# A two-expert kernel after windowed attention: the pools of PSUM banks are merged two feature ranges later

## Chip, cores, metric

The kernel runs on one core of a Trainium2 chip. The metric is device time in microseconds of one execution, the median of the runs shown. On the core, TensorE (PE) does matmuls and transposes into PSUM, VectorE (DVE) and ScalarE (ACT) read PSUM and do the elementwise work, GpSimd (POOL) and SyncE (SP) issue most of the transfers. Each engine takes its own instructions strictly in the order in which they were written to it, and waits on semaphores for the others.

## What is computed

```
scores = q @ k^T / 8, kept only where 0 <= i - j < 64       # 4 batches, 8 heads, 576 rows, 64 per head
x      = softmax(scores) @ v, heads side by side            # 2304 x 512
h      = x @ w_in ;  g = clamp-square of h ;  x2 = g @ w_out # 512 -> 2048 -> 512
h2     = x2 @ w_in2 ; solu = h2 * softmax(h2) ; layer norm, gain
out    = ln @ w_out2                                        # 512 -> 1024 -> 512
```

The function of h is (h + 1)^2 / 4 between -1 and 1, 0 below and h above. All is float32; the large products are made from three matmuls each of a high and a low part (hi*hi, hi*lo, lo*hi).

## The kernel before

The 2304 tokens are cut into six blocks of 384 (`NB`); a block is two attention tiles of 192 tokens, and a tile has four pairs of heads, so that a block needs eight attention units, numbered g. The first expert runs over the blocks j and, inside a block, over 16 ranges of 128 features, f. One step (j, f) is

- `moe_h` (L490): 12 matmuls of 384 columns that sum h for 128 features in one PSUM bank, tile `ps_h`, from the block's `xh` and `xl` (four chunks of 128 features of x, three matmuls each);
- `moe_g`, `moe_g2`, `moe_g3` (L500 to L515): ACT makes relu and square of it (L505, L506), DVE the clamp that reads the bank a last time (L511), ACT the high part `gh` (L512), DVE the low part `gl` (L515);
- `moe_y` (L518, L526): 12 matmuls, that add the step's contribution to the four sums `acc0` to `acc3` of the block, one bank each. After f = 15, `moe_out` copies the four sums out (`xo`, by ACT at L536 and DVE at L538) and POOL writes them to DRAM (L539); the copies have two buffers, so that the third and fourth wait until the first and second are written.

In this document h(j,f) and y(j,f) stand for the 12 matmuls of `moe_h` and of `moe_y`. The attention of later blocks is spread over the steps in small pieces (`slots`, L600): scores of a unit (`ps_s`, L352, and L442 in the form for two units together), their maximum by DVE (L360, L452), the exponential by ACT (L366, L458), the normalisation by DVE (L377, L378, L386), the transposes of the probabilities (`ps_p`, L402) with their copy by ACT (L407), and the product with v (`ps_x`, L421), which ACT and DVE turn into `xh` (L428) and `xl` (L429). Each of `ps_s`, `ps_p` and `ps_x` takes a PSUM bank for a while. Units 14 and 15 complete the x of block 1; their products with v run while the last steps of block 0 do.

PSUM has eight banks. Four are the sums. During block 0 the other four are two pools of two: `ps_at` for the attention pieces and `ps_h` for h. When these are closed, one pool `ps_ring` of four takes their banks, and attention pieces and h take turns in it; a tile of the new pool waits for what used its bank before. `at_bank` and `h_bank` (L95 to L106) take from the ring as soon as there is one.

The order on each engine isn't the order of the text: a list scheduler with a simulated time line places the instructions from their dependences, the banks among them, when the kernel is built. So a change of who may use which bank moves instructions.

Of the kernel before, what the change touches and what calls it, by code (L numbers as in the profile page):

```python
# [20 lines left out]
def kernel(  # L21
# [73 lines left out]
    def at_bank(name):  # L95
        if spare:
            spare.append(spare.pop(0))
            if spare[-1] is not None:
                return ps_acc.tile([128, 512], F32, tag=spare[-1], name=name)
        if ring:  # L100
            return ring[0].tile([128, 512], F32, tag="r", name=name)
        return ps_at.tile([128, 512], F32, tag="a", name=name)
# [47 lines left out]
    def w_conv(start=True):  # L150
        if w_b:
            split_c(*w_b.pop(0))
        if w_a:
            w_b.append(w_a.pop(0))
            split_b(*w_b[-1])
        if w_raw and start:
            w_a.append(w_raw.pop(0))
            split_a(*w_a[-1])
# [331 lines left out]
    def moe_h(j, f, c):  # L490
        ps = h_bank()[:, c]
        n = 0
        for kc in range(KC):
            hi, lo = wih[f][:, kc, :], wil[f][:, kc, :]
            for a, bb in ((hi, xh[j]), (hi, xl[j]), (lo, xh[j])):
                nc.tensor.matmul(ps, a, bb[:, kc, c], start=(n == 0), stop=(n == 3 * KC - 1))  # L496
                n += 1
        return ps

    def moe_g(part, ps):  # L500
        c = part[2]
        u = wk_p.tile([128, NB], F32, tag="u", name="u")[:, c]
        hi = wk_p.tile([128, NB], F32R, tag="gh", bufs=3, name="gh")[:, c]
        lo = wk_p.tile([128, NB], F32R, tag="gl", bufs=3, name="gl")[:, c]
        nc.scalar.activation(u, ps, ACTF.Relu, bias=half, scale=0.5)  # L505
        nc.scalar.activation(u, u, ACTF.Square)  # L506
        gh[part[0], part[1], part[2].start], gl[part[0], part[1], part[2].start] = hi, lo
        return ps, u, hi, lo

    def moe_g2(ps, u, hi, lo):  # L510
        g = nc.vector.scalar_tensor_tensor(u, u, 1.0, ps, op0=ALU.min, op1=ALU.max)  # L511
        return nc.scalar.copy(hi, u).ins, g.ins  # L512

    def moe_g3(j, ps, u, hi, lo):
        nc.vector.tensor_tensor(lo, u, as_f32(hi), op=ALU.subtract)  # L515
# [15 lines left out]
    def moe_out(j, es):  # L531
        for e in es:
            xo = wk_p.tile([128, NB], F32, tag="u" if j == NBLK - 1 and e > 1 else "xo", name="xo")
            a = acc.pop((j, e))[:, 0:NB]
            if e % 2 == 0:
                nc.scalar.copy(xo, a)  # L536
            else:
                nc.vector.tensor_copy(xo, a)  # L538
            nc.gpsimd.dma_start(out=x2d[j][e], in_=xo)  # L539
# [109 lines left out]
    def slot(n):  # L649
        for _ in range(n):  # L650
            next(stages, None)
# [7 lines left out]
    def x2_load(p):  # L659
        r = x2r[p] = d_p.tile([128, KC, 256], F32, tag="x2", bufs=2, name="x2r")  # L660
        c = 0
        while c < 256:
            j, c0 = divmod(256 * p + c, NB)
            n = min(256 - c, NB - c0)
            nc.sync.dma_start(out=r[:, :, c:c + n], in_=x2d[j][:, :, c0:c0 + n].rearrange("e p n -> p e n"))
            c += n
# [183 lines left out]
    for n in range(len(seq) + 2):  # L850
        if n < len(seq):
            j, f, c = seq[n]
            last = j == NBLK - 1
            n0 = n1 = 1
            if c == FIRST:
                z = na * (f + 1) // F0 - na * f // F0
                n0, n1 = z - z // 2, z // 2
            if j == 1 and f == 0:
                fr_ctx.close()
                ring.append(rg_ctx.enter_context(  # L860
                    tc.tile_pool(name="ps_ring", bufs=4, space=PSUM, reuse_waits="tile")
                ))
            if last and f == 8:
                rg_ctx.close()
                ring[0] = ps_ctx.enter_context(tc.tile_pool(name="ps_ring2", bufs=2, space=PSUM, reuse_waits="tile"))
            if last and f == 0:
                at_ctx.close()
                d_p = ctx.enter_context(tc.tile_pool(name="d", bufs=2, side="right", reuse_waits="tile"))
                x2_load(0)
            if j == 1 and f == 4:  # L870
                gl_row = wk_p.tile([128, NB], F32, tag="xo", name="gl_row")[0:DF2 // 128, 0:128]
                nc.sync.dma_start(
                    out=gl_row.rearrange("k (b i) -> k b i", b=4),
                    in_=g_ln.rearrange("(b k i) -> k b i", b=4, i=32),
                )
            if j == 1 and f == 7:
                ps = at_bank("ps_g")
                nc.tensor.transpose(ps[:, 0:DF2 // 128], gl_row, ident[0:DF2 // 128, 0:DF2 // 128])
                nc.vector.tensor_copy(gl_sb, ps[:, 0:DF2 // 128])
            part = moe_g(seq[n], moe_h(j, f, c))  # L880
        if n >= 1 and n - 1 < len(seq):
            moe_g3(seq[n - 1][0], *prev)
        if n < len(seq):
            prev = part
            slot(n0)
            w_conv()
            pins = moe_g2(*part)
        if n >= 2:
            jy, fy, cy = seq[n - 2]
            moe_y(jy, fy, cy)  # L890
            if fy == NF - 1:
                moe_out(jy, (0, 1))
        if n < len(seq):
            slot(n1)
            w_conv()
            if j == 0:
                w_load(2)
            w2_step(n, *pins)
            if last and f < 2:
                w2_vals(f)  # L900
            if last and f in (2, 3):
                w2_sums(f - 2)
            if last and f >= 2:
                with tc.issue_after(pins[0]):
                    w2_split(f - 2)
            if last and 2 <= f < 10:
                w2_load(f - 2)
        else:
            w_conv()
        if n >= 2 and fy == NF - 1:  # L910
            moe_out(jy, (2, 3))
        if n < len(seq):
            if last and f == 1:
                x2_load(1)
            if last and f == 5:
                with tc.issue_after(pins[0]), tc.issue_after(pins[1]):
                    x2_prep(0)
            if last and f in P_STEPS:
                st_p(0, P_STEPS[f])
            if last and f == 14:  # L920
                l2_norm(0)
            if last and f == 15:
                st_p(1, "P2")
        elif n == len(seq):
            x2_load(2)
            x2_prep(1)
            st_p(1, "P3")
            l2_norm(1)
# [66 lines left out]
```

## Time and profile before

| | us |
|---|---|
| median of 3 runs (703.43 to 706.93) | 703.74 |
| the profiled execution | 703.17 |
| its span on the core | 701.4 |
| PE busy | 678.1 (97%) |
| PE weight loads busy | 625.6 (89%) |
| DVE busy | 448.3 (64%) |
| ACT busy | 412.5 (59%) |
| POOL busy | 134.2 (19%) |

The profiled execution takes 1.8 us more than its span. Times below are from the start of the span. A busy PE is one that has a matmul in flight: matmuls overlap, so that the distance from one start to the next, not the length of one, tells how fast they go.

### The profile page before, as it was taken

To read this page: it belongs to the slowest core of one execution; us is meant where nothing else is said; L and a number is where in the kernel's file an instruction comes from. 1 tells how busy PE (TensorE), PEld (TensorE's weight loads), DVE (VectorE), ACT (ScalarE), POOL (GpSimd) and SP (SyncE) were. 2 spreads that over 40 slices of the span, in tenths; PEclk is the share of its full clock that TensorE was granted. 3 is DMA by queue.
4 is the path that set the end of the run, shared out by engine and by line. 5 is a ranking of instruction groups with operands and counts; after the bars stand their busy time and mean duration, and the time that the engine had idled before them with its cause. 6 is when DMAs were issued, how large, how long until landed. Compare 5 with 4: busy or idle time off the path is not lost.

```text
span 701.4 us, 12574 instructions
## 1 busy us (share of the span) xinstructions
PE 678.1 (97%) x4439; PEld 625.6 (89%) x4439; DVE 448.3 (64%) x1213; ACT 412.5 (59%) x1006; POOL 134.2 (19%) x178
## 2 busy tenths in 40 slices
PE   6899888899999999999999999999999999999998
PEld 5689788799999999999999999999997888888887
DVE  4789889646445555454455552643289999999850
ACT  5889777665656655665566565364455555445451
POOL 1112221100001000021112111662272322220000
PEclk9999999999999999999999999999999999999999
DMA  9996896625353523346351211562024455444331
GB/s 194 253 241 161 218 245 196 148 35 108 72 116 112 116 64 76 77 129 126 85 113 61 106 41 51 173 202 93 1 83 142 155 178 189 158 147 150 103 109 46
DMA packets 150551, 88.94 MB, mean 127 GB/s; under 512 B 118616, under 2 KB 134744, under 8 KB 150488
## 3 DMA queue, kind: packets, MB, share of 16 engines
q1 hardware_dynamic: 135160, 49.84, 30.2%
q0 software_dynamic: 12592, 33.57, 14.9%
q10 hardware_dynamic: 2736, 4.72, 1.8%
q8 instruction: 35, 0.57, 0.3%
q14 instruction: 28, 0.23, 0.1%
HBM read 63.97 MB, written 24.12 MB: 126 GB/s over the span
## 4 chain that ended last, share of the span: by engine, by line
PE 71%; issue 13%; POOL 4%; DVE 4%; DMA 3%; SPq 3%; ACT 2%; POOLq 0%; DVEq 0%
PE acc L526 21%; PE ps_h L496 21%; PE ps_o L827 14%; PE P L712 9%; DMA wst<-in_moe_w_in_dram 3%; POOL wil L249 2%; PE ps_x L476 2%; PE ps_s L442 2%; PE ps_p L402 2%; SPq L279 1%; DVE gl L515 1%; POOL wst L124 1%; SPq L302 1%; POOL wst L126 1%; DVE x2p L692 1%
## 5 line engine op out<-in xcount | busy, mean ns | idle before, releaser
L511 DVE SCALAR_TENSOR_TENSOR u<-u,ps_h 128x384 f32<-128x384 f32 (+1 forms) x98 | 53.3, 544 | 142.3 <-ACT u L506 141.4
L496 PE MATMUL ps_h<-xh,wih 128*128 128x384 f32 (+1 forms) x392 | 132.0, 337 | 3.1 <-ACT wih L145 3.0
L526 PE MATMUL acc<-gl,woh 128*128 128x384 f32 (+1 forms) x392 | 130.3, 334 | 2.1 <-DVE gl L515 2.1
L496 PE MATMUL ps_h<-xl,wih 128*128 128x384 f32 (+1 forms) x392 | 130.7, 334 | 0.4 <-DVE xl L429 0.4
L496 PE MATMUL ps_h<-xh,wil 128*128 128x384 f32 (+1 forms) x392 | 130.9, 334 | 0.0
L526 PE MATMUL acc<-gh,wol 128*128 128x384 f32 (+1 forms) x392 | 129.3, 332 | 0.0
L526 PE MATMUL acc<-gh,woh 128*128 128x384 f32 (+1 forms) x392 | 123.8, 341 | 2.3 <-ACT gh L512 2.3
L505 ACT ACTIVATE u<-ps_h,half 128x384 f32<-128x384 f32 (+1 forms) x98 | 56.1, 574 | 97.5 <-PE ps_h L496 97.3
L515 DVE TENSOR_TENSOR gl<-u,gh 128x384 fp32r<-128x384 f32 (+1 forms) x98 | 62.6, 640 | 35.2 <-ACT gh L512 34.6
L512 ACT CAST gh<-u 128x384 fp32r<-128x384 f32 (+1 forms) x98 | 49.7, 508 | 49.9 <-DVE u L511 34.8
L496 PEld LDWEIGHTS ps_h<-xh,wih 128*128 128x128 f32 x392 | 74.1, 189 | 4.5 <-ACT wih L145 3.6
L526 PEld LDWEIGHTS acc<-gh,woh 128*128 128x128 f32 x392 | 72.0, 188 | 6.2 <-ACT gh L512 3.5
L526 PEld LDWEIGHTS acc<-gl,woh 128*128 128x128 f32 x392 | 73.7, 188 | 3.1 <-DVE gl L515 2.7
L496 PEld LDWEIGHTS ps_h<-xl,wih 128*128 128x128 f32 x392 | 74.1, 189 | 1.0 <-DVE xl L429 0.8
L496 PEld LDWEIGHTS ps_h<-xh,wil 128*128 128x128 f32 x392 | 74.1, 189 | 0.1
L526 PEld LDWEIGHTS acc<-gh,wol 128*128 128x128 f32 x392 | 73.6, 188 | 0.1
L712 PE MATMUL P<-wih,x2p 128*128 128x512 f32 x216 | 71.6, 390 | 0.7 <-DVE x2p L692 0.7
L827 PE MATMUL ps_o<-woh,wol 128*128 128x512 f32 (+1 forms) x152 | 57.6, 379 | 0.0
L827 PE MATMUL ps_o<-woh,woh 128*128 128x512 f32 (+1 forms) x152 | 57.5, 379 | 0.0
L827 PE MATMUL ps_o<-wol,woh 128*128 128x512 f32 (+1 forms) x152 | 57.5, 378 | 0.0
L506 ACT ACTIVATE u<-u 128x384 f32<-128x384 f32 (+1 forms) x98 | 51.1, 522 | 1.9
L712 PEld LDWEIGHTS P<-wih,x2p 128*128 128x128 f32 x216 | 40.4, 188 | 9.2 <-DVE x2p L692 1.1
(123 smaller groups left out, 1191.8 us busy)
## 6 DMA issues: line engine op xcount, KB each, us to landing
wst<-in_moe_w_out_dram POOLq DMA_DIRECT2D x22, 512.0 KB, 7.4
wst<-in_moe_w_in_dram POOLq DMA_DIRECT2D x21, 512.0 KB, 5.5
vw<-in_v_dram SPq DMA_DIRECT2D x32, 256.0 KB, 5.3
lnd<-e SPq DMA_DIRECT2D x16, 512.0 KB, 2.7
lT<-lnd SPq DMA_DIRECT2D x64, 128.0 KB, 3.0
x2d<-xo POOLq DMA_DIRECT2D x24, 192.0 KB, 2.6
out_dram<-o ACTq DMA_DIRECT2D x17, 256.0 KB, 2.0
w2d<-w2st POOLq DMA_DIRECT2D x8, 512.0 KB, 3.0
```

The lines of the kernel that those rows point to most:

```text
L249: nc.gpsimd.tensor_tensor(lo, v_, as_f32(hi), op=ALU.subtract)
L402: nc.tensor.transpose(ps[:, i * 128:i * 128 + 128], p[:, i, :], ident)
L442: nc.tensor.matmul(ps[x][64 * c:64 * c + 64, i * 128 + c0:i * 128 + 128], z[r, KQ + i * 64:KQ + i * 64 + 64], z[r, i * 64 + c0:i * 64 + 12 ...
L496: nc.tensor.matmul(ps, a, bb[:, kc, c], start=(n == 0), stop=(n == 3 * KC - 1))
L505: nc.scalar.activation(u, ps, ACTF.Relu, bias=half, scale=0.5)
L506: nc.scalar.activation(u, u, ACTF.Square)
L511: g = nc.vector.scalar_tensor_tensor(u, u, 1.0, ps, op0=ALU.min, op1=ALU.max)
L512: return nc.scalar.copy(hi, u).ins, g.ins
L515: nc.vector.tensor_tensor(lo, u, as_f32(hi), op=ALU.subtract)
L526: nc.tensor.matmul(acc[j, e][:, c], a, bb, start=(f == 0 and n == 0 and c.start == 0), stop=(f == NF - 1 and n == 2),)
L712: nc.tensor.matmul(ps, l, r, start=(n == 0), stop=(n == 5))
L827: nc.tensor.matmul(ps, a[kk // 4][:, kk % 4, :], b[kk][:, c:c + w], start=(n == 0), stop=(n == 3 * NK2 - 1),)
```

## The change

The two pools of block 0 stay open for the steps (1,0) and (1,1); the ring of four is opened at (1,2).

```diff
-            if j == 1 and f == 0:
+            if j == 1 and f == 2:
                 fr_ctx.close()
                 ring.append(rg_ctx.enter_context(
                     tc.tile_pool(name="ps_ring", bufs=4, space=PSUM, reuse_waits="tile")
                 ))
```

No instruction is added or removed, and none changes its shape. The scheduler orders a stretch anew that begins at the last step of block 0 and ends with the transposes `ps_p_2129`; from there on the engines' orders are the same but for a swap of two neighbours on ACT and one on PE. Three places follow. In the names, `wih_146` and `wil_147` are the weights of f = 0, `wih_168` and `wil_169` those of f = 1, `woh_150` belongs to y(1,0), `wol_173` to y(1,1), `acc_751` to `acc_754` are the sums of block 0, `acc_2047` to `acc_2050` those of block 1.

PE before, from the scores of unit 16 on (the first row):

```order
L352 MATMUL ps_s<-kq_124 128x128 x3
L421 MATMUL ps_x<-pT,vw 64x64 x6
L402 MATMUL ps_p<-ident,p 128x128 x3
L352 MATMUL ps_s<-kq_125 128x128 x3
L496 MATMUL ps_h<-xh,wih_146 128x384
L496 MATMUL ps_h<-xl,wih_146 128x384
```

PE now, from the last of y(0,15) to the first of y(1,0); the transposes `ps_p` are those of the third row above:

```order
L526 MATMUL acc_754<-gh,wol_1409 128x384
L496 MATMUL ps_h<-xh,wih_146 128x384
L496 MATMUL ps_h<-xh,wih_168 128x384
L496 MATMUL ps_h<-xl,wih_146 128x384
L496 MATMUL ps_h<-xh,wil_147 128x384
L496 MATMUL ps_h<-xl,wih_168 128x384
L496 MATMUL ps_h<-xh,wil_169 128x384
L402 MATMUL ps_p<-ident,p 128x128 x3
L352 MATMUL ps_s<-kq_125 128x128 x3
L421 MATMUL ps_x<-pT,vw 64x64 x6
L526 MATMUL acc_2047<-gh,woh_150 128x384
```

Before, these transposes came right behind the scores and the product with v of another unit, with all of h(1,0) after them. Now the 24 matmuls of h(1,0) and h(1,1) are done ahead of them, 14 of these also ahead of the scores of the first row, and behind them come scores, a product with v and y(1,0).

ACT before, from the copy of the third sum of block 0 on:

```order
L536 COPY xo_2010<-acc2_753 128x384
L407 COPY pT_1825<-ps_p_1824 128x384
L366 ACTIVATE p_1831,sm_1833<-p_1831,mx_1832 128x128 x3
L505 ACTIVATE u_1861<-ps_h_1848,half_69 128x384
L428 CAST xh_1895<-ps_x_1897 128x192
```

ACT now, the same stretch:

```order
L536 COPY xo_2005<-acc2_753 128x384
L505 ACTIVATE u_1856<-ps_h_1843,half_69 128x384
L505 ACTIVATE u_1932<-ps_h_1919,half_69 128x384
L506 ACTIVATE u_1856<-u_1856 128x384
L506 ACTIVATE u_1932<-u_1932 128x384
L407 COPY pT_1825<-ps_p_1824 128x384
L512 CAST gh_1857<-u_1856 128x384
L366 ACTIVATE p_1831,sm_1833<-p_1831,mx_1832 128x128 x3
```

The copy `pT_1825`, which the product `ps_x` waits for, stood first and now stands behind four operations on h.

PE now, from the end of y(1,1) on, with the transposes and the product with v of unit 17:

```order
L526 MATMUL acc_2050<-gh,wol_173 128x384
L402 MATMUL ps_p<-ident,p 128x128 x3
L421 MATMUL ps_x<-pT,vw 64x64 x6
L442 MATMUL ps_s<-kq_124 64x128
L442 MATMUL ps_s<-kq_125 64x128
```

Before, h(1,1) stood between these transposes and this product, and the first ten matmuls of y(1,0) between the pair scores (`ps_s`, L442) and h(1,2). Now nothing stands between any of them. The scores go on for ten more rows, those of tile `ps_s_1947` first and those of `ps_s_1948` behind; then follows h(1,2) with `ps_h_2016`, the first tile of the ring, which waits for DVE, while the second, `ps_h_2073`, waits for nothing. On DVE the three maxima of `ps_s_1947` come first, then a transpose of q and k (L317), then the three of `ps_s_1948`.

## Rows read from the trace of the kernel before

**Rows 1.** Windows: PE, PEld, DVE, ACT, POOL busy us (instructions), clock, DMA share, GB/s.
```profile
130.00:134.00 4.00, 1.65 (x22) 1.35 (x21) 2.89 (x12) 2.06 (x9) 1.24 (x4) 1.00 0.84 207
```

**Rows 2.** Waits of PE from 145 us to the end: us, times, longest.
```profile
PE acc L526 <- DVE gl L515: 1.3, 1, 1.3
PE P L712 <- DVE x2p L692: 0.7, 1, 0.7
```

**Rows 3.** Timeline of PE around the gap: start, us, what, [idle before].
```profile
129.40 0.83 PE L352 MATMUL ps_s<-kq 128*128 128x128 f32 x6
130.16 0.71 PE L421 MATMUL ps_x<-pT,vw 64*64 64x64 f32 x12
133.23 0.52 PE L402 MATMUL ps_p<-ident,p 128*128 128x128 f32 x3 [2.35 <-DVE p L386]
133.58 0.83 PE L352 MATMUL ps_s<-kq 128*128 128x128 f32 x6
134.32 0.44 PE L496 MATMUL ps_h<-xh,wih 128*128 128x384 f32 x1
```

**Rows 4.** Timeline of DVE and of ACT in and behind the gap.
```profile
132.52 0.56 DVE L386 TENSOR_TENSOR p<-p,rs 128x384 f32<-128x384 f32 x1
...
133.78 0.48 ACT L407 COPY pT<-ps_p 128x384 f32<-128x384 f32 x1 [1.34 <-PE ps_p L402]
```

**Rows 5.** Timeline: last matmul of h(1,0) on PE, then ACT behind it.
```profile
136.33 0.34 PE L496 MATMUL ps_h<-xh,wil 128*128 128x384 f32 x1
...
136.71 0.58 ACT L505 ACTIVATE u<-ps_h,half 128x384 f32<-128x384 f32 x1 [0.65 <-PE ps_h L496]
137.22 0.32 ACT L428 CAST xh<-ps_x 128x192 fp32r<-128x192 f32 x1
137.43 0.53 ACT L506 ACTIVATE u<-u 128x384 f32<-128x384 f32 x1
137.86 0.47 ACT L407 COPY pT<-ps_p 128x384 f32<-128x384 f32 x1
```

**Rows 6.** Timeline of DVE, a stretch without idle time.
```profile
140.71 0.36 DVE L429 TENSOR_TENSOR xl<-ps_x,xh 128x192 fp32r<-128x192 f32 x1 [1.03 <-ACT xh L428]
141.14 0.55 DVE L511 SCALAR_TENSOR_TENSOR u<-u,ps_h 128x384 f32<-128x384 f32 x1
141.61 0.64 DVE L317 STREAM_TRANSPOSE kq<-qk 128x448 f32<-128x448 f32 x1
142.17 0.25 DVE L452 CUSTOM_DVE_ANT_0 p<-ps_s,mask 128x128 f32<-128x128 f32 x1
...
143.41 0.55 DVE L515 TENSOR_TENSOR gl<-u,gh 128x384 fp32r<-128x384 f32 x1
```

**Rows 7.** Timeline of PE: transposes, a product with v, pair scores of two units.
```profile
137.21 0.52 PE L402 MATMUL ps_p<-ident,p 128*128 128x128 f32 x3
...
139.75 0.57 PE L421 MATMUL ps_x<-pT,vw 128*64 128x64 f32 x12
140.25 0.89 PE L442 MATMUL ps_s<-kq 64*64 64x128 f32 x24
```

**Rows 8.** Timeline of PE: first matmul of h(1,2); transposes behind h(1,4).
```profile
142.91 0.33 PE L496 MATMUL ps_h<-xh,wih 128*128 128x384 f32 x1
...
151.58 0.82 PE L402 MATMUL ps_p<-ident,p 128*128 128x128 f32 x6
```

**Rows 9.** Sums of block 0: copy (ACT), write (POOL); landings, issues 129.4 and 132.7.
```profile
128.56 0.48 ACT L536 COPY xo<-acc 128x384 f32<-128x384 f32 x1 [0.52 <-PE acc L526]
131.98 0.46 ACT L536 COPY xo<-acc 128x384 f32<-128x384 f32 x1
...
129.44 1.10 POOL L539 DMA_DIRECT2D x2d<-xo  x2 [13.14 <-ACT xo L536]
...
DMA to landing us min/median/max: 2.2/2.2/2.2
...
DMA to landing us min/median/max: 5.1/5.1/5.1
```

**Rows 10.** Windows near the start, columns as in rows 1.
```profile
30.00:33.30 3.30, 1.83 (x20) 1.14 (x19) 2.75 (x8) 3.30 (x12) 0.00 (x0) 0.95 1.09 175
33.30:36.30 3.00, 3.00 (x23) 2.83 (x23) 2.13 (x7) 2.98 (x9) 0.54 (x1) 0.50 0.53 79
```

## The prediction

> **What bounds the kernel.** I read the page first: PE is busy for 97% of the span, so whatever stops PE moves the end, and whatever doesn't is hidden. Next I read where PE waits. From 145 us to the end it waits twice, for 1.3 and 0.7 us [rows 2]; a delay that PE has at 145 us can be given back nowhere but there. Then the stretch that the change orders anew. In 130 to 134 us PE is busy for only 1.65 us [rows 1], and the timeline shows why: the product with v starts at 130.16, and the transposes behind it start at 133.23 after an idle 2.35 us [rows 3]. They wait for DVE's normalisation, which runs from 132.52 and ends at 133.08 [rows 4]. The 12 matmuls of h(1,0) stand behind these transposes in PE's order, since their bank is the one that the transposes fill: h starts at 134.32, just after ACT has emptied that bank (133.78 + 0.48 = 134.26) [rows 3, 4]. This is the only large gap of PE in the stretch.
>
> **What the change removes.** With the old pools open, h(1,0) and h(1,1) have two banks of their own, so that the 24 matmuls no longer queue behind the transposes. One matmul costs 0.1734 us: 50 of them fill 142.91 to 151.58 [rows 8]. Counted along the new order, the scores that stood at 129.40 have 14 matmuls of h put ahead of them and 3 of y(0,15) put behind, net 11 x 0.1734 = 1.91 us; with 0.2 for four more changes between small and large matmuls (a first large matmul behind small ones starts its successor 0.28 later and not 0.17: 134.32 in rows 3 is followed at 134.60) they start at 131.5. From these scores to the transposes the chain through DVE and ACT took 133.23 - 129.40 = 3.83 us [rows 3], so the transposes can start at 135.33. PE meanwhile does the product with v (starts 0.76 behind the scores [rows 3], takes 0.65) and 13 large matmuls (2.26 us and 0.1), until 135.27. The gap of 2.35 shrinks to 0.06. Gain: **2.3 us**.
>
> By the Trainium skill's page Perfetto Trace Analysis, section Optimization Strategy, a gap that repeats on the engine that should be busy can mean that too little PSUM is there for the next tile. By that rule the sum would end here, at 703.17 - 2.3 = 700.9; here the gap comes once, and what ends it is DVE and not a freed bank, so I count on.
>
> **What the change adds.** The 24 matmuls were the cover of the steps behind. I follow the new order with durations from the rows.
>
> 1. *Product with v of unit 16.* PE has transposes at 135.33 and the scores of unit 17 0.35 later, which take 0.74 [rows 3], and is ready for the product at 136.42. It needs ACT's copy of the transposes, now behind four operations. The last matmul of h(1,0) starts at 134.75, that of h(1,1) at 135.10; ACT starts relu 0.38 behind a last matmul (136.33 to 136.71), the next operation follows relu after 0.51 and square after 0.43 [rows 5]. So relu at 135.13 and 135.64, square at 136.15 and 136.58, the copy at 137.01 to 137.48, the product at 137.54 (+0.06 as in rows 3 and 4). PE idles **1.12 us**.
> 2. *Low part of g(1,0).* The product ends at 138.05; three matmuls of y(1,0) use the high part and end at 138.65. The fourth needs DVE's low part. DVE's order is clamp (after the square, 136.71), three maxima, a transpose, the clamp of h(1,1), the low part. Its pitches are 0.47 for a clamp, 0.56 for the transpose, 0.62 for three maxima (half of 142.17 to 143.41), 0.55 for the low part [rows 6]: 136.71 + 0.47 + 0.62 + 0.56 + 0.47 + 0.55 = 139.38. PE idles **0.75 us**. Then 21 matmuls of y run through, 3.64 us, to 143.07; their other inputs are ready a microsecond before they are needed.
> 3. *Product with v of unit 17.* It stands directly behind its transposes (143.15). ACT's copy starts 0.65 behind these and takes 0.47 (137.21, 137.86 [rows 5, 7]), so the product starts at 144.33, where the transposes were done at 143.5. PE idles **0.8 us**; before, h(1,1) filled this.
> 4. *Pair scores.* The first tile's scores follow after 0.5 (139.75 to 140.25 [rows 7]) and take 0.41. The second tile's bank is that of the product, which DVE leaves 140.71 + 0.36 - 139.75 = 1.32 after its start [rows 6, 7], at 145.65. PE idles **0.45 us**.
> 5. *h(1,2).* In the two attention banks, taken in turn, the transposes that h(1,0) waited for before, the product of unit 17 and the second tile of pair scores share one. That bank is the ring's first again, and h(1,2) waits for DVE, h(1,3) for nothing: it is the second tile's maxima that h(1,2) waits for. DVE starts 0.43 behind the start of its low part of x (145.29 + 0.43 = 145.72), then three maxima, a transpose, three maxima: 0.62 + 0.56 + 0.62, until 147.52, with a hand-over of 0.06 147.58. PE was done with the scores at 146.1 and idles **1.5 us**; before, ten matmuls of y(1,0) stood there.
>
> From there 36 matmuls of h (6.24 us and 0.1) bring PE to the transposes of unit 18 at 153.9; it was there at 151.58 with the same work done [rows 8]. That is 2.3 later; by the waits, 0.06 + 1.12 + 0.75 + 0.8 + 0.45 + 1.5 = 4.7 of new idle time against 2.35 of old, also **+2.3 us**. The small swaps behind this stand beside PE's work and cost nothing as long as PE doesn't wait there [rows 2]. Transfers on SP (queries, keys and v of later units) are issued some 2 us later; their units come several steps later, so that nobody waits for them. POOL's four writes of block 0's sums move too (rival D).
>
> Each of the new waits has 0 below. Step 1 can grow by a late write of the sums (up to 2.5, rival D), steps 2 to 5 by little, since each is a chain of measured pieces.
>
> **Sum.** 703.17 (profiled execution) + 2.3 = 705.5; that execution lies 0.57 below the median of three, against which it would be 706.0. I say 705.8.
>
> **Rivals.**
> - *B, the gap goes and the new waits don't come.* 703.17 - 2.35 = 700.8 at best, about 703 with half of the waits. For it: each wait is short, and ACT and DVE are far from full in the stretch. Against it: in steps 1, 3 and 5 PE's next instruction reads or overwrites just what the chain makes.
> - *C, the clock falls.* From 143.5 to 147.6 PE works for some 1.3 us and idles in three pieces. Near the start PE was busy for 1.83 of 3.3 us, and in the 3.0 us behind, at full work, its granted clock was 0.50, that is 1.2 in place of 2.4 GHz [rows 10]. Against it: in 130 to 134 us, with 1.65 busy of 4, the clock stayed at 1.00 [rows 1]. If it fell, 3.0 us of full work at half speed cost 1.5: 705.5 + 1.5 = 707.0. The Trainium skill's TensorE: Matmul & The Clock Gate, section A second HAM failure mode: psum-queue depth-cycling, says that a PE that idles briefly between groups while cycling through PSUM banks swings between the two clock levels. The trace has both outcomes.
> - *D, the sums' write lands late (slower).* The third sum's copy on ACT waits until the first is in DRAM, and now relu of h(1,0) and all of step 1 stand behind this copy. The first copy started 0.84 ahead of the scores (128.56, 129.40 [rows 3, 9]); three matmuls fewer stand between now, 0.52, so it starts at 131.18, and POOL issues 0.88 behind its start (129.44 [rows 9]), at 132.06. Landing took 2.2 us for this write and 5.1 for the third, that was issued into the loads of v [rows 9]. These loads reuse buffers that the product of unit 15 frees: it began 0.72 behind the issue before (130.16), 0.2 behind it now (132.26). With 2.2 the write is there at 134.26; the third copy, which stood 2.58 behind the scores (131.98) and could go at 134.08, ends at 134.72, 0.4 before relu. With 5.1 it ends at 137.16 + 0.46 = 137.62, relu is 2.5 late and so is step 1: 705.5 + 2.5 = 708.0. It costs something from a landing of 2.6 on, and puts the time over half a per cent from 4.4 on.
> - *E, nothing moves the end.* The waits are as long as the gap: 703.2 to 704.2. It needs half of the new waits to be hidden, and I see no cover for them.
>
> **Numbers.** Half a per cent, 3.5 us, is what a measurement of this kernel can tell from no change. Forecast 0.62, B 0.08, C 0.12, D 0.08, E 0.10. Of D half, of C a third and a little of the forecast's upper end lie above 707.3: slower 0.12. Faster needs under 700.2, more than the whole gap: 0.02. Same: 0.86. The range of 8 in 10 leaves out B, and the upper half of D: 703.4 to 707.5.
>
> **What would show it.** Right: the wait of the transposes for DVE's normalisation gone, and PE waiting in 136 to 148 us for ACT's copy of the transposes (twice, about 1.1 and 0.8), for DVE's low part of g (0.8), and before h(1,2) for DVE's maxima (1.5), with the transposes behind h(1,4) near 153.9 and everything later shifted by that. Wrong: those transposes at 149 (B), a granted clock under 1.00 behind 143 us (C), a landing above 4 us of the first sum's write with ACT idle before the third sum's copy (D).

## The result and the profile after

| | before | changed |
|---|---|---|
| median, first comparison (8 runs each) | 704.88 | 710.02 (708.28 to 711.95) |
| median, repeated (21 and 11 runs) | 705.15 | 709.36 |
| profiled execution, its span | 703.17, 701.4 | 711.32, 709.5 |
| PE busy | 678.1 | 685.0 (97%) |
| PE weight loads busy | 625.6 | 631.9 (89%) |
| DVE, ACT busy | 448.3, 412.5 | 446.9, 411.9 |

The change makes the kernel slower: ratio 1.007, 95% interval 1.0048 to 1.0092; repeated, 1.0061, 1.0042 to 1.008. The forecast was 705.8 with a range up to 707.5, so it had the sign and missed the size. Of the 21 executions of before in the repeated comparison one was a slow one, of 1698 us, and is outside the ratio. PE is busy 6.9 us longer with the same instructions.

The waits of PE in the changed kernel, first from 120 to 162 us, then from 162 us to the end (us, times, longest):

```profile
PE ps_x L421 <- ACT pT L407: 2.6, 2, 2.0
PE ps_h L496 <- DVE mx L452: 1.4, 1, 1.4
PE acc L526 <- DVE gl L515: 0.6, 1, 0.6
...
PE acc L526 <- DVE gl L515: 1.3, 1, 1.3
PE P L712 <- DVE x2p L692: 0.6, 1, 0.6
```

The wait for DVE's normalisation [rows 3] is gone, and waits named in the prediction stand in its place (the one inside the pair scores isn't listed; the timeline below shows it). The last two rows are those of [rows 2]: nothing is given back later.

The timeline of PE (start, us, what, [idle before]):

```profile
133.00 0.83 PE L352 MATMUL ps_s<-kq 128*128 128x128 f32 x6
133.76 0.71 PE L421 MATMUL ps_x<-pT,vw 64*64 64x64 f32 x12
...
136.79 0.50 PE L402 MATMUL ps_p<-ident,p 128*128 128x128 f32 x3
137.13 0.83 PE L352 MATMUL ps_s<-kq 128*128 128x128 f32 x6
139.96 0.57 PE L421 MATMUL ps_x<-pT,vw 128*64 128x64 f32 x12 [2.00 <-ACT pT L407]
...
141.86 0.63 PE L526 MATMUL acc<-gl,woh 128*128 128x384 f32 x1 [0.61 <-DVE gl L515]
142.29 0.52 PE L526 MATMUL acc<-gh,wol 128*128 128x384 f32 x1
142.61 0.52 PE L526 MATMUL acc<-gl,woh 128*128 128x384 f32 x1
...
148.24 0.57 PE L421 MATMUL ps_x<-pT,vw 128*64 128x64 f32 x12 [0.57 <-ACT pT L407]
148.74 1.75 PE L442 MATMUL ps_s<-kq 64*64 64x128 f32 x24
151.93 0.43 PE L496 MATMUL ps_h<-xh,wih 128*128 128x384 f32 x1 [1.44 <-DVE mx L452]
...
152.48 0.52 PE L496 MATMUL ps_h<-xh,wil 128*128 128x384 f32 x1
152.80 0.52 PE L496 MATMUL ps_h<-xh,wih 128*128 128x384 f32 x1
...
159.82 0.82 PE L402 MATMUL ps_p<-ident,p 128*128 128x128 f32 x6
```

The transposes at 136.79 follow without idle time, against 2.35 in [rows 3]. Then come the five steps: 2.00 before the product of unit 16, 0.61 for the low part, 0.57 before the product of unit 17, 0.86 inside the pair scores (1.75 long, against 0.89 in [rows 7]), 1.44 before h(1,2). Behind the second and the last of them the large matmuls start 0.32 apart (142.29, 142.61; 152.48, 152.80) and not 0.1734.

Windows of the changed kernel (PE, PEld, DVE, ACT, POOL busy us, clock, DMA share, GB/s):

```profile
136.80:140.00 3.20, 1.20 (x12) 1.01 (x11) 0.84 (x4) 2.71 (x7) 0.54 (x1) 1.00 1.07 240
...
142.00:145.20 3.20, 3.20 (x11) 3.20 (x12) 1.72 (x6) 0.09 (x1) 1.08 (x2) 0.50 0.60 141
145.20:147.20 2.00, 2.00 (x13) 1.96 (x12) 0.00 (x0) 0.00 (x0) 0.00 (x0) 0.96 0.93 225
147.20:152.00 4.80, 2.79 (x41) 2.03 (x39) 2.56 (x15) 2.67 (x11) 0.00 (x0) 1.00 0.12 18
152.00:155.60 3.60, 3.60 (x12) 3.60 (x13) 1.83 (x7) 0.66 (x4) 0.00 (x0) 0.53 0.31 50
155.60:162.00 6.40, 6.40 (x40) 6.37 (x40) 2.23 (x4) 4.78 (x10) 0.00 (x0) 1.00 0.23 37
```

The same columns for the kernel before, and the row of PE's timeline with the scores that stand ahead of all of this, first before, then now:

```profile
129.00:151.00 22.00, 19.61 (x163) 18.37 (x162) 14.57 (x53) 13.19 (x43) 2.73 (x5) 1.00 0.57 130
...
121.51 0.83 PE L352 MATMUL ps_s<-kq 128*128 128x64 f32 x6
...
123.10 0.83 PE L352 MATMUL ps_s<-kq 128*128 128x64 f32 x6
```

Before, the granted clock stayed at 1.00. Now it fell to 0.50 and to 0.53 (the mean of a window; the lower level is 1.2 GHz), each time just when PE had work again. What was lost is (1 - 0.50) x 3.2 = 1.6 and (1 - 0.53) x 3.6 = 1.7 us. What the change costs lies here: from these scores, the only ones there at 128x64 in sixes, to the transposes behind h(1,4) [rows 8] it took 30.07 us and now takes 36.72. I call this **the stretch**. Behind it both kernels need 549.7 to 549.8 us to the end of the span. Ahead of it the instructions are the same; in this trace of the changed kernel it starts 1.59 us later than before, in the repeated one 1.36 earlier (120.15), so that this part is scatter. Of the 6.65 us, new idle time is 2.00 + 0.61 + 0.57 + 0.86 + 1.44 - 2.35 = 3.1, and the clock 3.3; 0.2 is left over.

### The profile page after: what moved, and what is told of

It is laid out like the page before. It is cut to its first block, busy times and chain, and to the rows that moved or that the text cites. A ratio compares the mean times of both kernels' runs of the same rounds, so it can differ in the third digit from the quotient of the medians.

```text
span 709.5 us, 12572 instructions
## 1 busy us (share of the span) xinstructions
PE 685.0 (97%) x4439; PEld 631.9 (89%) x4439; DVE 446.9 (63%) x1213; ACT 411.9 (58%) x1006; POOL 134.2 (19%) x178
## 4 chain that ended last, share of the span: by engine, by line
PE 76%; issue 11%; POOL 4%; DVE 4%; ACT 3%; DMA 2%; SPq 0%; POOLq 0%; DVEq 0%
PE acc L526 22%; PE ps_h L496 22%; PE ps_o L827 14%; PE P L712 9%; POOL wil L249 2%; PE ps_x L476 2%; PE ps_s L442 2%; PE ps_p L402 2%; PE ps_s L352 1%; DVE gl L515 1%; PE ps_x L421 1%; DMA wst<-in_moe_w_in_dram 1%; ACT p L366 1%; DMA vw<-in_v_dram 1%; PE ps_t L334 1%
## 5 line engine op out<-in xcount | busy, mean ns | idle before, releaser
L496 PE MATMUL ps_h<-xl,wih 128*128 128x384 f32 (+1 forms) x392 | 132.3, 338 | 0.4 <-DVE xl L429 0.4
L496 PE MATMUL ps_h<-xh,wil 128*128 128x384 f32 (+1 forms) x392 | 132.4, 338 | 0.0
L515 DVE TENSOR_TENSOR gl<-u,gh 128x384 fp32r<-128x384 f32 (+1 forms) x98 | 61.3, 627 | 34.0 <-ACT gh L512 33.5
```

## Experiments

All ratios are to the kernel before, from runs on the same chip. The stretch comes from each kernel's trace; the clock is the mean granted clock over all runs of a kernel (before: 0.9925 over 111 runs). The runs come from several sets, in which before had medians of 704.88 to 705.91; so a difference of about 1 us between two medians of the table can come from the set, and the ratios are the safer comparison. The diffs show the lines that act; the names that they wait for are set in lines that are left out (...): `cp` at a unit's copy of the transposes, `tr` at its transposes, `ps_last` and `s_last` at its scores.

| kernel | median | ratio, 95% interval | stretch, us | clock |
|---|---|---|---|---|
| changed, first comparison | 710.02 | 1.007, 1.0048 to 1.0092 | 36.72 | 0.990 |
| changed, repeated | 709.36 | 1.0061, 1.0042 to 1.008 | 36.07 | 0.990 |
| 1 copy first | 710.29 | 1.0067, 1.0045 to 1.0089 | 35.42 | 0.989 |
| 2 y(1,1) later | 707.25 | 1.0025, 1.0011 to 1.0039 | 35.65 | 0.993 |
| 3 filled | 708.08 | 1.0033, 1.002 to 1.0047 | 33.92 | 0.995 |
| 4 copy first, y(1,1) later | 708.28 | 1.0037, 1.0018 to 1.0056 | 33.14 | 0.991 |
| 5 writes on SP | 708.44 | 1.0056, 1.0034 to 1.0078 | 33.42 | 0.991 |
| 6 other buffers for two sums | 707.40 | 1.0028, 1.0009 to 1.0046 | 33.52 | 0.992 |
| 7 y(1,1) later, filled | 705.98 | 1.0012, 0.9999 to 1.0026 | 32.76 | 0.994 |
| 8 ring at (1,1) | 705.87 | 1.001, 0.9992 to 1.0028 | 30.97 | 0.994 |
| 9 ring at (1,3) | 706.52 | 1.0011, 0.9993 to 1.003 | 35.58 with y(1,2) | 0.993 |
| 10 before, y(0,15) later | 703.55 | 0.9971, 0.9951 to 0.999 | 29.12 | 0.994 |
| 10 repeated | 703.38 | 0.9973, 0.9957 to 0.999 | 29.13 | 0.994 |
| 11 the same, other buffers | 703.42 | 0.9973, 0.996 to 0.9986 | 29.16 | 0.994 |
| 12 changed, y(0,15) later | 710.27 | 1.0064, 1.0041 to 1.0087 | 35.18 | 0.990 |

**1. Copy first.** Relu and square of h(1,0) are put behind ACT's copy of the transposes of unit 16.

```diff
...
-            part = moe_g(seq[n], moe_h(j, f, c))
+            ph = moe_h(j, f, c)
+            if j == 1 and f in (0,):
+                with tc.issue_after(cp[16]):
+                    part = moe_g(seq[n], ph)
+            else:
+                part = moe_g(seq[n], ph)
```

> Changed kernel, but ACT's relu and square of h(1,0) are queued behind its copy of the transposes of unit 16. Theory (the new waits of the stretch, one late write, and two falls of PE's clock that the waits bring on): the 2.0 us wait before the product of unit 16 falls to under 0.5, the 0.57 before the product of unit 17 goes because eight matmuls of y(1,0) now stand between, the fall of the clock behind it (1.6 us) goes; the wait of h(1,2) stays at 1.4. Time 4 us (3 to 5) under the changed kernel's. Rival (the waits alone, the clock falls by chance): 2 to 2.5 us under it.

A miss: the time is that of the changed kernel, where 3 to 5 us less were expected. PE's waits from 120 to 162 us in this kernel (its line numbers are one higher), and the row of ACT's timeline ahead of the copy:

```profile
PE acc L527 <- ACT gh L513: 3.0, 1, 3.0
PE ps_h L497 <- DVE mx L453: 1.4, 1, 1.4
PE ps_x L422 <- ACT pT L408: 0.6, 1, 0.6
```

```profile
139.25 0.48 ACT L537 COPY xo<-acc 128x384 f32<-128x384 f32 x1 [2.01 <-DMA x2d<-xo]
```

Step 1 shrank from 2.00 to 0.65, and the three microseconds stand one instruction on, before y(1,0): its high part now comes behind the copy, relu, square and the exponentials. In this order too, then, ACT's chain sets the time. The wait of unit 17's product is gone, and one clock fall is left of two, behind the wait of 2.97 (0.50 in 146 to 148 us). And ACT stands idle 2.01 us for a write ahead of the copy of the third sum: that is rival D.

**2. y(1,1) later.** It is put behind the pair scores, as ten matmuls of y(1,0) were before the change.

```diff
...
-            moe_y(jy, fy, cy)
+            if jy == 1 and fy == 1:
+                with tc.issue_after(ps_last[PU]):
+                    moe_y(jy, fy, cy)
+            else:
+                moe_y(jy, fy, cy)
```

> Changed kernel, but y(1,1) is queued behind the pair scores of units 18 and 19, so that its 12 matmuls stand between these and h(1,2). Theory: the 1.4 us wait of h(1,2) goes and the fall of the clock at h(1,2) (1.6 us) goes with it, the earlier waits and the earlier fall stay: 3 us under the changed kernel's time (2 to 3.5). Rival (waits alone): 1.4 us under it.

The wait of 1.44 is gone, and the time lies 2.8 us under the changed kernel of the first comparison (2.1 under the repeated one). In the profiled execution the first clock fall lasted 9.4 us and not 3.2, over the pair scores and into y(1,1), so that the stretch shows only 1.1 of that, and whether the second fall went with its wait can't be read from this trace. A window of this kernel, columns as above:

```profile
139.50:148.90 9.40, 8.24 (x53) 7.09 (x52) 4.58 (x19) 3.09 (x13) 1.08 (x2) 0.50 0.50 113
```

**3. Filled.** The changed kernel with 22 matmuls more that compute nothing that is used: 11 behind the scores of unit 17, 3 behind the transposes of unit 17, 8 behind the pair scores.

```diff
...
+    def filler(ps, n, behind):
+        with tc.issue_after(behind):
+            for _ in range(n):
+                nc.tensor.matmul(ps[:, 0:NB], wih[0][:, 0, :], xh[1][:, 0, :], start=True, stop=True)
...
+            if j == 1 and f == 1:
+                if 11:
+                    filler(ps_acc.tile([128, 512], F32, tag="acc0", bufs=1, name="fill"), 11, ps_last["s", 17])
+                fl = ps_h.tile([128, 512], F32, tag="h", name="fill")
+                if 3:
+                    filler(fl, 3, tr[17])
+                filler(fl, 8, ps_last[PU])
```

> Changed kernel with 22 extra matmuls of 384 columns that nobody reads, put where PE waits: 11 before the product of unit 16, 3 before that of unit 17, 8 before h(1,2). They are 0.2 us shorter in sum than each wait, so the waits end when they did. Theory: the granted clock stays at 1.00 from 136 to 160 us, no matmul there starts 0.32 us after the one before it, and the time is 1.5 to 3.1 us under the changed kernel's although nothing else gets faster. Rival (clock falls by chance, not from these waits): the same time as the changed kernel, or up to 0.5 us more.

A window of this kernel, columns as above:

```profile
134.00:156.00 22.00, 20.95 (x157) 19.14 (x156) 11.09 (x41) 11.78 (x37) 1.62 (x3) 1.00 0.51 117
```

PE does more work and the kernel is 1.3 to 1.9 us faster than the changed one: the clock stays at 1.00 in the stretch, and the stretch is 2.8 shorter (2.2 against the repeated trace). Over its 11 runs the mean clock is 0.995, over the 19 of the changed kernel 0.990. So the falls come with PE's idle time, and they are a cost of their own beside the waits.

**4. Copy first and y(1,1) later**, the edits of 1 and 2 together.

> Both pins of copy_first and y11_cover together. Theory: no wait of PE over 0.6 us is left in the stretch and the clock stays; the 2.35 us gap of the kernel before is gone too, so the time is 1 to 2 us under the kernel before. Rival (waits alone, clock by chance): about 3.5 us under the changed kernel, that is 1 to 2 us above the kernel before.

A miss as well. The wait of 1.44 went, but that of 2.96 before y(1,0) stayed, as in 1, and the clock fell behind it (0.50 in 142 to 144 us).

**5. Writes on SP.** Block 0's sums are written from SP's queue.

```diff
-            nc.gpsimd.dma_start(out=x2d[j][e], in_=xo)
+            (nc.sync if j == 0 else nc.gpsimd).dma_start(out=x2d[j][e], in_=xo)
```

> The changed kernel, with the four writes of block 0's sums issued by SP and not by POOL, on a queue of their own; nothing else is meant to change. Theory (1.0 us of step 1 is the late write): the write is issued earlier behind its copy than POOL's 0.88, the third copy on ACT starts 0.5 to 1 us earlier, the wait before the product of unit 16 falls from 2.0 to 1.0 to 1.5, and the time from 0.5 to 1 us, or up to 2.5 if the first clock fall goes with it. Rival (the landing is slow because the loads of v stand in front of it, whoever issues): landing stays at 3.5 or is longer, no gain. Rival (clock falls come with any waits of this sum): step 1 shorter by a microsecond, both falls to 0.50 stay, ten or eleven matmuls at 0.32.

Inconclusive. The four landings had a median of 2.8 us instead of 3.6 and step 1 lost its wait, but the third and fourth copies still waited 1.1 and 2.0 us for the writes; DVE's normalisation of unit 16 now stood behind the fourth, and the transposes waited 1.90 for it: another place for the wait. In its profiled execution the clock stayed at 1.00 although the wait of 1.44 was there; over its runs it was 0.991.

**6. Other buffers for two sums.** The third and fourth copies go to the buffers of the low part of g, and wait for no write.

```diff
-            xo = wk_p.tile([128, NB], F32, tag="u" if j == NBLK - 1 and e > 1 else "xo", name="xo")
+            if j == 0 and e > 1:
+                xo = wk_p.tile([128, NB], F32, tag="gl", bufs=3, name="xo")
+            else:
+                xo = wk_p.tile([128, NB], F32, tag="u" if j == NBLK - 1 and e > 1 else "xo", name="xo")
```

> The changed kernel with the third and fourth sums of block 0 copied into two buffers of the low part of g, so that the third copy on ACT waits for no write; the scheduler then sets it behind the exponentials of unit 17. Theory (1.0 us of step 1 is the late write): relu of h(1,0) starts as soon as its matmuls are done, ACT's copy of the transposes of unit 16 one microsecond earlier, the wait before the product of unit 16 falls from 2.0 or 2.1 to 0.5 to 1.1, and the time by 0.9 to 1.5 us; if the first clock fall goes with it, by up to 3. The waits of unit 17's product (0.57) and of h(1,2) (1.44) stay. Rival (the write isn't what ACT waits for): the wait stays at 2.0, no gain.

The timeline of PE, and below it windows of the same kernel:

```profile
139.72 0.57 PE L421 MATMUL ps_x<-pT,vw 128*64 128x64 f32 x12 [0.97 <-ACT pT L407]
...
141.27 0.44 PE L526 MATMUL acc<-gh,woh 128*128 128x384 f32 x1 [0.43 <-ACT xo L539]
...
149.49 0.66 PE L496 MATMUL ps_h<-xh,wih 128*128 128x384 f32 x1 [1.44 <-DVE mx L452]
```

```profile
141.30:146.30 5.00, 5.00 (x37) 4.49 (x37) 2.27 (x7) 1.42 (x5) 1.62 (x3) 1.00 0.80 185
...
149.50:153.50 4.00, 4.00 (x14) 4.00 (x15) 1.90 (x7) 0.75 (x5) 0.00 (x0) 0.58 0.31 49
```

Step 1 is 0.97 without the write, where the prediction had 1.12, and 2.00 with it: the late write was worth 1.0 us. The edit also lets the scheduler set the third copy behind that of the transposes, and y(1,0) waits 0.43 for it; its own 0.48 ahead of relu would have fitted into the time that ACT stood idle for the write. In this trace the first clock fall went and the second stayed. The stretch is 3.2 us shorter (2.6 against the repeated trace), the median 2.0 to 2.6.

**7. y(1,1) later, filled**: the edit of 2, with the first 14 of the matmuls of 3.

```diff
...
+            if j == 1 and f == 1:
+                if 11:
+                    filler(ps_acc.tile([128, 512], F32, tag="acc0", bufs=1, name="fill"), 11, ps_last["s", 17])
+                fl = ps_h.tile([128, 512], F32, tag="h", name="fill")
+                if 3:
+                    filler(fl, 3, tr[17])
```

> The changed kernel with y(1,1) placed behind the pair scores (no wait of 1.44 before h(1,2)), and with 14 matmuls that compute nothing used in PE's idle time: 11 behind the scores of unit 17, 3 behind the transposes of unit 17. Theory (waits and clock falls are two costs that add, and the second comes from the first): the granted clock stays at 1.00 in 130 to 160 us, the stretch is 36.1 to 36.7 less 3.1 (clock) less 1.44 (wait) = 31.5 to 32.3 us, and the time 1 to 2 us over before (ratio 1.0015 to 1.003), that is 3 to 4 under the changed kernel. Rival (the matmuls that fill cost as much as the falls): 707 or more, no better than placing y(1,1) alone.

A window of this kernel, columns as above:

```profile
138.00:156.00 18.00, 16.82 (x128) 14.99 (x127) 10.61 (x40) 10.26 (x34) 1.59 (x3) 1.00 0.55 116
```

The clock stayed at 1.00 and the stretch is 32.76, half a microsecond above the expected; the time is 0.6 us above before, which can't be told from it, and 3.4 to 4.0 under the changed kernel. Taking the clock falls and one wait away thus gives back most of the loss.

**8 and 9. The ring one range earlier, or later.**

```diff
-            if j == 1 and f == 2:
+            if j == 1 and f == 1:
```

> The changed kernel with the ring opened one feature range earlier, at (1,1). h(1,0) alone can go ahead of the transposes; h(1,1) goes back between the transposes of unit 17 and their product, y(1,0) stays ahead of them, and y(1,1) is mixed into h(1,4). Theory (every matmul moved forward as cover is missing behind): step 1 of the prediction is smaller, as one relu and square stand ahead of ACT's copy and not two (0 to 0.6 instead of 2.0), step 3 (product of unit 17, 0.57) is 0, steps 2 and 5 (low part 0.6, maxima 1.4) stay; one clock fall instead of two. Stretch 32 to 33.5, that is 3 to 4.5 us under the changed kernel (36.7) and 2 to 3 over before (30.1). Rival (only the late write matters): step 1 stays at 2.0 and the stretch at 36 or more.

```diff
-            if j == 1 and f == 2:
+            if j == 1 and f == 3:
```

> The changed kernel with the ring opened one feature range later, at (1,3). Order up to the scores of unit 17 as in the changed kernel, then h(1,2) before the product of unit 16, y(1,0) and y(1,1), the transposes of unit 17, y(1,2), its product, pair scores, h(1,3). Theory (cover moves, waits follow it): the wait of product 16 for the copy (2.0) goes, since 12 matmuls of 2.08 us stand there; the wait of product 17 (0.57) goes; the wait for the last maxima (1.44) stays, now at h(1,3); the granted clock may fall once, behind that one. Stretch with the 12 matmuls of y(1,2) inside it: 30.1 + 2.1 + 1.4 - 2.3 + late write 0 to 1 = 31.3 to 32.3, and one clock fall 1.5 more; in total 2.5 to 5 us under the changed kernel, the same as before within 2. Rival (banks held longer are worse): time at or above the changed kernel's.

PE's waits from 119 to 162 us, first with the ring at (1,1), then at (1,3):

```profile
PE acc L526 <- ACT gh L512: 1.8, 1, 1.8
PE ps_h L496 <- ACT xh L428: 0.9, 1, 0.9
```

```profile
PE ps_h L496 <- DVE u L511: 1.6, 1, 1.6
PE ps_h L496 <- DVE mx L452: 1.4, 1, 1.4
```

With the ring at (1,1) the stretch is 30.97, better than expected, but with other waits than expected: those of steps 1, 3 and 5 are gone, y(1,0) waits 1.8 for its high part, and h waits 0.9 for `xh`. At (1,3) the waits of steps 1 and 3 are gone, and one of 1.6 for the bank of h(1,0) is new. Without y(1,2), 12 x 0.1734 = 2.1 us, its stretch is 33.5, with one clock fall behind the wait of 1.4. Neither can be told from before; each order has two uncovered waits in place of the gap.

**10. Before, with y(0,15) later.** The pools are as before the change. The 12 matmuls of y(0,15), which stood ahead of the scores of unit 16, are put behind them, into the gap.

```diff
...
-            moe_y(jy, fy, cy)
+            if jy == 0 and fy == NF - 1:
+                with tc.issue_after(s_last[16]):
+                    moe_y(jy, fy, cy)
+            else:
+                moe_y(jy, fy, cy)
```

> The kernel before with one edit: y(0,15) is placed behind the scores of unit 16 and the product of unit 15, where PE idled 2.35 us [rows 3]; all later cover of the kernel before (h(1,0), h(1,1), ten matmuls of y(1,0)) stays where it is. Theory (the gap is only badly covered, and the merge of the pools costs by spending the later cover): the gap closes to 0.3 or less, no new wait of over 0.5 us comes up to the transposes behind h(1,4), the granted clock stays at 1.00 in 130 to 150 us, the stretch from the scores of unit 16 to those transposes is 30.0 + 2.08 (twelve matmuls of y now inside it) - 2.2 = 29.9 us, and 12 matmuls less stand ahead of it: 1.5 to 2.2 us under before, ratio 0.997 to 0.998. Rival (late write): the four sums are copied 2 us later, so their writes and ACT's third copy hold up relu of h(1,0) and the copy of the transposes, and the gain is under 0.5. Rival (first gap is needed anyway): y(0,15) ahead of the scores only delays, 0.

> The kernel before with y(0,15) behind the scores of unit 16, again, on another chip perhaps, to settle whether it is the fastest of the three. Theory: 1.5 to 2.5 us under before (ratio 0.9965 to 0.998), stretch 30.5 to 31.0 with 12 matmuls more inside it, idle before the transposes of unit 16 of 0.58. Rival (the first result was chance): ratio 0.999 to 1.001.

PE's timeline in the repeated run, the idle time of the stretch:

```profile
128.37 0.94 PE L353 MATMUL ps_s<-kq 128*128 128x128 f32 x6 [0.36 <-DVE xl L430]
...
132.81 0.52 PE L403 MATMUL ps_p<-ident,p 128*128 128x128 f32 x3 [0.58 <-DVE p L387]
```

With 11 this is the fastest kernel of the study, 1.8 to 2.3 us under before in both comparisons, though by less than half a per cent. The gap of 2.35 became 0.58, with 0.36 ahead of the scores, and no wait came behind. The expected lengths of the stretch were wrong, since y(0,15) lies inside it in both kernels: it is 0.94 shorter. The rest of the gain, about 1 us, goes along with a higher mean clock, 0.994 for 0.9925 (0.0015 x 704 = 1.1 us at most). That before loses clock behind its gap in some executions would explain it, but is not shown: neither of its two traces has it.

**11. The same with the buffers of 6.**

> The kernel before with y(0,15) behind the scores of unit 16 and with the two buffers of the low part of g for the third and fourth sums. Theory: in the order of the kernel before nothing on PE waits for these writes, so this adds nothing to placing y(0,15) late: 1.5 to 2.5 us under before, within 0.7 us of that kernel. Rival (late copies of the sums hold up something there too): 0.7 us or more under that kernel.

No further gain: in this order nobody on PE waits for the writes.

**12. Changed, with y(0,15) later**: the edit of 10 on the changed kernel.

> The changed kernel with y(0,15) placed behind the scores of unit 16 as well: both the pools kept open and the gap covered by y(0,15). h(1,0) and h(1,1) are still placed early, y(1,1) partly falls between the pair scores and h(1,2). Theory (PE has one stock of matmuls that are ready, and each can cover one wait): with the gap covered by y(0,15), h(1,0) and h(1,1) placed early cover nothing, and the waits for the copy of transposes, the high part of g(1,0) and unit 17's copy stay uncovered: 1.5 to 4 us of them, so 1 to 4 us above the kernel that only places y(0,15) late, and within 2 us of before. Rival (only the gap and h(1,2) ever mattered): as fast as that kernel or faster, 2 or more under before.

PE's waits from 119 to 162 us, and a window behind them:

```profile
PE ps_p L403 <- ACT u L507: 2.5, 1, 2.5
PE acc L527 <- ACT gh L513: 0.4, 1, 0.4
```

```profile
142.00:148.00 6.00, 6.00 (x37) 5.36 (x36) 2.99 (x13) 1.79 (x8) 1.08 (x2) 0.51 0.74 187
```

Worse than expected: 6.9 us above kernel 10. The edit that gains 2 us with the old order of the pools gains nothing with the new one. h(1,0) and h(1,1) still go early, so that ACT has their relu among the exponentials of unit 17; PE's transposes of that unit wait 2.5 us, and the clock falls behind that wait. The profile lays the wait on ACT's square of h, which ended at 140.45; what these transposes read is DVE's normalisation, which ended at 140.41 and itself came behind those exponentials.

**Both kernels again.** The kernels before and changed, as they are.

> The kernel before once more, for a second trace: what in its time is scatter. Theory: the stretch from the scores in front of it to the transposes behind h(1,4) is 30.1 us again within 0.3, with the gap of 2.35 in it within 0.2 and clock 1.00 there; what differs between two executions lies in clock falls ahead of 120 us, which shift the stretch's start by up to 3 us. Rival: the gap itself sometimes drops the clock, and the stretch is 31.5 or more.

> The changed kernel once more, for a second trace and more times on one chip beside before. Theory (4.9 us = 2.3 waits of PE + 1.0 late write + some 1.6 of clock): the waits in the stretch are the same within 0.2 us (2.0, 0.6, 0.6, 1.4), the granted clock falls below 0.70 at least once in 140 to 157 us, and over the runs the mean granted clock is 0.0015 to 0.0035 under that of before, which at half speed is 1.0 to 2.5 us in one or two microseconds of work for each 0.0014 to 0.0028. Ratio 1.005 to 1.009. Rival (the two clock falls of the first profile were chance): clock 1.00 through the stretch, mean clock of the runs as before, stretch 33.5 and not 36.7.

The stretch of before is 30.07 again, to the hundredth, with its gap of 2.35 and the clock at 1.00. What differs between these two executions of before lies ahead of it. In the changed kernel the waits came again (2.14, 0.20, 0.57, 0.86 and 1.44), and both falls:

```profile
138.00:141.00 3.00, 2.79 (x9) 2.29 (x9) 2.91 (x9) 1.28 (x6) 1.08 (x2) 0.50 0.42 73
...
148.50:151.50 3.00, 2.95 (x9) 2.98 (x10) 1.96 (x7) 0.78 (x5) 0.00 (x0) 0.50 0.32 52
```

## Why the prediction was right and wrong

The step that failed is the sum. It put the granted clock and the late write at nothing and left them to rivals C and D, with chances of 0.12 and 0.08. Both came, and together: the write cost 1.0 us, and the clock 3.3 in the profiled execution and up to 1.8 by the mean over all runs. The waits that the forecast did count came much as predicted.

- *The gap.* Right: 2.35 before, none now, and the product of unit 15 and the scores stand where the count along the order put them.
- *Step 1*, mis-sized: 1.12 predicted, 2.00 measured, 0.97 with the write out of the way (6). Its working for rival D gave the price from the landing, and that was right: it costs something from 2.6 us on. Only the landing was wrong. The forecast took 2.2 of [rows 9]; it was 3.6. The rows of the writes in the changed kernel, and ACT behind the first of them:

```profile
L539 POOL DMA_DIRECT2D x2d<-xo x4: 540/542/559, 133.6 to 142.6; - x4
...
DMA to landing us min/median/max: 2.2/3.6/3.7
```

```profile
132.67 0.48 ACT L536 COPY xo<-acc 128x384 f32<-128x384 f32 x1 [2.27 <-PE acc L526]
...
137.29 0.48 ACT L536 COPY xo<-acc 128x384 f32<-128x384 f32 x1 [1.60 <-PE ps_p L402]
137.66 1.06 ACT L505 ACTIVATE u<-ps_h,half 128x384 f32<-128x384 f32 x2
138.60 0.94 ACT L506 ACTIVATE u<-u 128x384 f32<-128x384 f32 x2
139.42 0.49 ACT L407 COPY pT<-ps_p 128x384 f32<-128x384 f32 x1
```

  Issued at 133.6 and landed some 3.6 us later, the first write frees its buffer at 137.2, and the third copy starts at 137.29. The profile lays that wait on PE's transposes, which came at about the same time. In the repeated trace, as in run 1, it names the write for the same copy:

```profile
134.47 0.48 ACT L536 COPY xo<-acc 128x384 f32<-128x384 f32 x1 [1.74 <-DMA x2d<-xo]
```

- *Steps 2 to 5*: 0.75, 0.8, 0.45 and 1.5 predicted, 0.61, 0.57, 0.86 and 1.44 measured, 3.50 against 3.48 together. Following each new wait down its chain of measured pieces found them all, mostly within 0.25; that the sums agree to 0.02 is luck, since step 4 was about twice its size, step 3 was smaller, and step 2 was 0.20 in the repeated trace. The bank of step 4 came free when predicted (DVE's read of the product ended at 149.57, 1.33 behind the product's start, against 1.32); why the scores took 0.4 longer beside that is open.
- *Rival C failed by its chance.* The forecast gave a clock fall 0.12, because behind the one gap of [rows 1] the clock had stayed at 1.00. It came twice in both traces. Its working looked at 143.5 to 147.6 alone, that is at the later fall; the one behind steps 1 and 2 was not in it, and in 6, with step 1 near its predicted size, that one did not come. Its price, 1.5, was right for each: ten matmuls 0.32 apart lose 10 x (0.32 - 0.173) = 1.5. The rule of the Trainium skill's page TensorE: Matmul & The Clock Gate, section A second HAM failure mode: psum-queue depth-cycling, that brief idle time between groups makes a PE that cycles through PSUM banks swing between its two clock levels, agrees with both traces of the changed kernel (1.00, 0.50, 0.96, 1.00, 0.53, 1.00 in the windows of the first).
- *C and D were weighed as rivals of the forecast, one at a time.* They were additions to it, and not independent, since a late write lengthens the very wait that the clock falls behind (with the write out of the way, in 6, the first fall was gone too). Their own prices added up, 705.8 + 1.0 + 2 x 1.5, give 709.8. That this meets the 709.4 to 710.0 measured is in part luck, since the base lay higher too.
- *The base.* The first three times of before had a median of 703.74; the later sets have 704.9 to 705.9. Some 1.1 us of the miss of 4.2 is that, and no part of the mechanism. Against before, the forecast was +2.1 to +2.3 and the result +4.2 to +5.1.

The sum for the median then is: new idle time 3.1, with the late write's 1.0 in it, and of the clock at most what the mean over runs gives, (0.9925 - 0.990) x 705 = 1.8; together up to 4.9, against 4.2 to 5.1 measured. The clock's part is a bound, since a fall need not delay the end by all that it loses: of the 111 executions of before, the 42 with a mean clock of 0.990 have a median only 2.1 us above that of the 12 with 0.998 (705.76, 703.68), where 0.008 x 705 is 5.6. At a like clock the two kernels still differ: with 0.992 or 0.993, six executions of the changed kernel have a median of 709.28 and 37 of before 705.92, which is 3.4 us, near the idle time alone. In the two profiled executions of the changed kernel the clock took 3.1 to 3.3 in the stretch; how the falls are spread over runs without a trace stays open.

By the Trainium skill's page Perfetto Trace Analysis, section Optimization Strategy, a repeating gap can mean too little PSUM for the next tile. Here two banks kept for h did close the gap, and the kernel got slower. What the gap lacked was matmuls that were ready, and y(0,15) brought it from 2.35 to 0.58 without another bank (10).

## What to carry to other kernels

A gap closed with matmuls from further on opens where these stood: ask which waits they covered, and look first for work from ahead of the gap that covers none. Several short waits in a row can cost more than their sum, because the granted clock may fall behind them; price that as part of the forecast wherever the new order sets several waits close behind one another. And rivals that can come together are to be added, not chosen among.

## What was not expected of the hardware

- One idle piece of 2.35 us followed by transposes, scores and large matmuls left the clock at 1.00 in both traces of before, while 1.44 us, behind a product with v and pair scores, was followed by a fall in both traces of the changed kernel, in 6 and in 9, but not in 1 or 5. No one row here tells which.
- Falls were not equally long: 3.2 and 3.6 us at about 0.5 in the changed kernel, at least 6 us at 0.51 in 12, 9.4 us at 0.50 in 2.
- Matmuls whose result nobody uses, put into idle time of PE, made the changed kernel faster: 22 of them by 1.3 to 1.9 us, with a mean clock of 0.995 for 0.990.
- The same small write, 128x384, landed 2.2 to 5.1 us after its issue in one execution of before, and 2.2 to 3.7 in one of the changed kernel; what made the difference was not isolated.
